# Low states on half the contraction rows: two heads of the state product side by side on TensorE, and a new order plan

## The chip, the cores and the metric

The kernel runs on one core of a Trainium2 chip. The metric is device time in microseconds (us) of one execution; the kernel before has a median of 700.57 us over 3 runs (700.18 to 702.35). The core has TensorE (PE in the profile, its weight loads on a row of their own, PEld), VectorE (DVE), ScalarE (ACT), GpSimd (POOL, almost unused here) and the queue of SyncE (SP), which issues all DMAs.

## The reference, cut to what matters

```python
B, H, S, Ns, D = 8, 8, 512, 32, 64          # x: B,H,S,D   state: B,H,Ns,D
a     = softmax(scale * x @ state^T)         # over the 32 states
xread = a @ state
a2    = softmax(scale * state @ x^T)         # over the 512 tokens
sread = a2 @ x
x     = concat([xread, sread], axis=2)       # 544 tokens a batch, 8 heads x 64
out   = ((x @ w_a) * (x @ w_b)) @ w_out      # 512 -> 1536 -> 512, float32
```

`xread @ w_a` is never formed through `xread`. Since `xread = a @ state`, the kernel multiplies the states of every head by that head's 64 rows of `w_a` and `w_b` first (the **state product**) and lets the attention weights `a` act on the result. The state product is what the change touches.

## The kernel before, in words

**Precision.** A float32 operand is split into a high part in TensorE's fast one-pass format (fp32r) and a low part, the rest. A product of two split operands is then three matmuls (high by high, high by low, low by high).

**Chunks.** The 1536 hidden columns are six chunks of 256. For each chunk, `w_a` and `w_b` together are 512 columns (the index `x` below). `weights(c, hp)` loads the 128 rows of a pair `hp` of heads (4 pairs) as raw 8-byte values, and `Conv` turns them into high and low float32 parts: one ACT `mul`, five DVE instructions, and copies into the tile `wq` of 128 rows by 2 heads by 512. In `conv_w`, head 0's high part stands in rows 64 to 127 and its low part in rows 0 to 63 of `wq[:, 0]`; head 1's high part stands in rows 64 to 127 and its low part in rows 0 to 63 of `wq[:, 1]`. The states (`sd_h` high, `sd_l` low) stand twice, in rows 0 to 63 and again in rows 64 to 127, so one matmul over all 128 rows adds (state times high weight) and (state times low weight).

**The state product.** `project(c, hp, bg, hh)` makes, for one head `hh` and one group `bg` of four batches, two such matmuls (`sd_h`, then `sd_l`) into one PSUM bank, `ms`; ACT copies the bank to SBUF, and after the second head two DMAs write the pair to scratch in DRAM (`scr`). The `sd_l` matmul of 128 rows also adds low state times low weight. `ms` has two banks, shared with the attention's small products. Each of the chunks 1 to 5 has 16 `project` calls (4 pairs, 2 heads, 2 groups) of two 512-column matmuls; chunk 0 is held in another layout, with 256-column matmuls.

**The MLP.** For a batch and 128 hidden columns, `layer1` reads the state product back (`p_raw<-scr`), splits it (`p_h`, `p_l`) and multiplies with the attention weights (`at_h`, `at_l`) into two `ab` banks; ACT and DVE multiply the two halves and split the result (`g_h`, `g_l`); `layer2` multiplies with `w_out` into four `acc` banks. `VISITS` says which batch takes which chunks in which order, since chunks become ready one after another.

**What sets the order.** Nothing runs in the order in which it is written. A `Recorder` notes all instructions as units (a `with rec.together` block is one unit, whose matmuls follow each other), `Recorder.cost` gives each unit a cost, and `plan` lists them by due times. Due times go backwards from a pace that the MLP's matmuls set, and `SHIFTS` (unit number: hundreds of ns) moves single units. The resulting order of each engine is fixed in the program.

Of the kernel before, what the change touches and what calls it, by code (L numbers as in the profile page):

```python
# [10 lines left out]
F32 = mybir.dt.float32  # L11
F32R = mybir.dt.float32r
# [8 lines left out]
P = 128  # L21
# [24 lines left out]
WIDE = (0, 1)  # L46

JOINED = 3

# [118 lines left out]
class Recorder:  # L168
# [31 lines left out]
    def cost(self, u, eng, method, out, ins, kw):  # L200
        n = 1
        sh = (out if isinstance(out, View) else ins[0]).where()[0]
        for x in sh[1:]:
            n *= x
        ps = bool(ins) and ins[0].tile.pool.name.startswith("ps")
        if eng == "PE":
            if method == "transpose" or kw.get("is_transpose"):
                o = n * .85
            elif ins[-1].dtype == F32R:
                o = (n + 32) / 2.4  # L210
            else:
                o = n / .6
            if sh[0] < P:
                o *= sh[0] / P
            if method == "matmul" and "is_transpose" not in kw and ins[-1].dtype == F32 and not u.turned:
                o, u.turned = o + 370, True
            lat = o + 172
        elif eng == "ACT":
            if method == "activation":
                o, lat = (870, 960) if "accum_out" in kw else (560, 660)  # L220
            elif ps:
                o, lat = 466 * n / 512 + (60 if n < 300 else 0), 587 * n / 512 + (80 if n < 300 else 0)
            else:
                o, lat = 522 * n / 512, 100 + n * 1.015
            if n < 8:
                o, lat = 60, 80
        elif eng == "DVE":
            if method.startswith("tensor_scalar") and not ps:
                o, lat = (65, 140) if n <= 1 else (75, 166) if n <= 16 else (333 * n / 512, 419 * n / 512)
            elif method == "tensor_reduce":  # L230
                o, lat = 593, 676
            elif method == "transpose":
                o, lat = 628, 704
            elif method == "reciprocal":
                o, lat = (72, 154) if n == 1 else (162, 244)
            else:
                o, lat = 65 + n * 1.045, 155 + n * 1.045
        elif eng == "SP":
            o = 440
            v = out if isinstance(out, View) else ins[0]  # L240
            u.bytes = 4
            for x in v.where()[0]:
                u.bytes *= x
            u.load = isinstance(out, View) and out.tile.pool.name != "dram"
            u.serve, u.land = u.bytes / 428 + (0 if u.load or u.bytes < 4e5 else 240), 1560 if u.load else 900
            lat = 980 + u.serve + u.land
        else:
            o, lat = 1000, 1060
        if eng in ("ACT", "DVE") and out.tile.name.startswith("sd_") and len(out.where()[0]) == 4:
            o, lat = 2 * o, 2 * lat  # L250
        if eng in ("ACT", "DVE"):
            o, lat = o * SLACK, lat * SLACK
        if u.calls[:-1]:
            u.lat = u.occ + lat
            u.occ += o
        else:
            u.occ, u.lat = o, lat
# [8 lines left out]
class Engine:  # L266
# [13 lines left out]


SHIFTS = {
# [12 lines left out]
}  # L295


# [164 lines left out]
def attn_moe(ctx, tc, xt, xn, sd, wl, w_out, out):  # L462
    base = tc.nc
    rec = Recorder()
# [7 lines left out]
    def pool(name, bufs, free=False, **kw):  # L472
        p = Pool(ctx.enter_context(tc.tile_pool(name=name, bufs=bufs, **kw)), name, bufs, free)
        pools.append(p)
        return p
# [4 lines left out]
    proj = pool("proj", 2)  # L480
# [8 lines left out]
    def f32(ap):  # L489
        return ap.bitcast(F32)  # L490
# [28 lines left out]
    class Conv:  # L519
# [15 lines left out]
        def run(self):  # L535
            raw, t1 = self.raw, self.t1
            his, los = self.parts()
            t2 = proj.tile([P, 512], I32, name="t2")
            nc.vector.tensor_scalar(out=t2, in0=t1, scalar1=3, scalar2=0x7FFFF000,
                                    op0=ALU.logical_shift_left, op1=ALU.bitwise_and)  # L540
            nc.vector.scalar_tensor_tensor(out=t2, in0=raw[:, :, 1], scalar=-(1 << 31), in1=t2,
                                           op0=ALU.bitwise_and, op1=ALU.bitwise_or)
            for rows, o in his[:1]:
                nc.scalar.copy(out=o, in_=f32(t2[rows]))

            nc.vector.tensor_scalar(out=t1, in0=t1, scalar1=3, scalar2=0xFFF,
                                    op0=ALU.logical_shift_left, op1=ALU.bitwise_and)
            nc.vector.scalar_tensor_tensor(out=f32(t1), in0=raw[:, :, 0].bitcast(U32), scalar=2.0 ** -29,
                                           in1=t1, op0=ALU.mult, op1=ALU.add)
            pw = raw.rearrange("p a b -> p (a b)")[:, :512]  # L550
            nc.vector.tensor_scalar(out=pw, in0=t2, scalar1=-(1 << 23), scalar2=None, op0=ALU.bitwise_and)
            for rows, o in los[:1]:
                nc.vector.scalar_tensor_tensor(out=o, in0=f32(t1[rows]), scalar=2.0 ** -23,
                                               in1=f32(pw[rows]), op0=ALU.mult, op1=ALU.mult)
            for o, i in los[1:]:
                nc.scalar.copy(out=o, in_=f32(i))
            for rows, o in his[1:]:
                nc.scalar.copy(out=o, in_=f32(t2[rows]))

    nxt = []  # L560


    LO, HI, ALL = slice(0, D), slice(D, P), slice(0, P)

    sd_h = [proj.tile([P, 4, 2, P], F32R, name=f"sd_h{j}", bufs=1) for j in range(2)]
    sd_l = [proj.tile([P, 4, 2, P], F32R, name=f"sd_l{j}", bufs=1) for j in range(2)]
# [16 lines left out]
    scr = [[dram.tile([NG, 4, 4, NS, 512], F32, name=f"scr{c}_{g}") for g in range(2)] for c in range(NC)]  # L583
    w = {}

    def conv_w(src, *key):


        def parts():
            t = w[key] = proj.tile([P, 2, 512], F32R, name="wq", bufs=4)  # L590
            return ((HI, t[HI, 1]), (LO, t[HI, 0])), ((ALL, t[:, 0]), (t[LO, 1], t[HI, 0]))
        return Conv(src, parts, 2)

    def weights(c, hp):

        if c:
            return conv_w(wl[2 * c:2 * c + 2, :, hp, :].rearrange("f p x -> p f x"), c, hp)
        f, g = hp // 2, hp % 2
        return conv_w(wl[f, :, 2 * g:2 * g + 2, :], 0, f, g)

# [6 lines left out]

    st = {"n": 0}
    SW = ("sw_st", 2), ("wo10", 1), ("sw_st", 2), ("wo11", 1)

    def project(c, hp, bg, hh, psp, tag):
        if hh == 0:
            name, bufs = SW[st["n"] % len(SW)]
            st[bg], st["n"] = proj.tile([P, 2, 512], F32, name=name, bufs=bufs), st["n"] + 1
# [179 lines left out]
    class Batch:  # L794
        n, nk = S, NG
# [80 lines left out]
    class States:  # L876
        n, nk, begun = B * NS, 4, False
# [127 lines left out]
    def attend(b):  # L1005
        if b not in a_t:
            new_a(b)
        for g in range(NG):
            a = atts[b, g]
            a.load()  # L1010
            if b >= JOINED:
                end_reads(a.scores)
# [27 lines left out]

    def products(c, bg, where=ms):
        for hp in range(4):
            for hh in range(2):
                project(c, hp, bg, hh, *where)
        flush()
# [79 lines left out]
    order, start = plan(rec.units, pools, T0)  # L1125
# [46 lines left out]
```

## Time and profile before

| | |
|---|---|
| median of 3 runs | 700.57 us |
| the profiled execution's own time | 700.03 us |
| its span in the profile | 698.2 us |
| PE busy | 677.7 us (97%), 3712 instructions |
| DVE busy | 486.5 us (70%), 947 instructions |
| ACT busy | 394.3 us (56%), 727 instructions |
| granted TensorE clock | 0.999 |
| DMA | 134.36 MB, mean 192 GB/s |

The span is the time from the first to the last instruction; the execution's own time is 1.8 us longer, for what lies around it. PE's busy share counts the modelled length of each matmul (about 0.39 us for 512 columns) where successive matmuls start 0.23 us apart, so a busy PE is read from the starts of its matmuls. All instructions are issued from one helper line (L1129 before, L1162 after), so groups are told apart by the names of tiles: `ms<-wq,sd_l` is a state product with low states, `ab<-...` is layer 1, `acc<-wo,...` layer 2, `ms<-x_raw` and `ms<-x_nat,a` are attention's products. A form such as `128*32` is rows by columns of the weights that the matmul uses.

### The profile page before, as it was taken

The page shows a single profiled execution, that of the slowest core. Times are in us where ns is not written, and L with a number is a line of the kernel's source. Part 1 is how long each engine was busy: PE and PEld are TensorE (multiplying, and loading weights), DVE is VectorE, ACT ScalarE, POOL GpSimd, SP SyncE. Part 2 cuts the span into 40 slices and gives each one's busy share as a digit, 9 for nine tenths or more (in the row PEclk, how much of TensorE's full clock was granted, in tenths as well). Part 3 has the DMA queues.
Part 4 walks back from the last instruction along what each step waited for, and adds up shares of the span by engine and source line. Part 5 has one row for each costly group of instructions (what it writes and reads, how often), then busy time and mean ns, then how long its engine had stood idle before and what let it go on. Part 6 is the DMA issues. An engine that isn't in the chain of part 4 may idle for free.

```text
span 698.2 us, 10183 instructions
## 1 busy us (share of the span) xinstructions
PE 677.7 (97%) x3712; PEld 543.2 (78%) x3712; DVE 486.5 (70%) x947; ACT 394.3 (56%) x727; POOL 0.7 (0%) x6
## 2 busy tenths in 40 slices
PE   4899999999999999999999999999999999999997
PEld 1576767887878888788888877877798888988886
DVE  5999788889986775745997367558869734884321
ACT  6988967898764667754543344334555433552322
POOL 0000000000000000000000000000000000000000
PEclk9999999999999999999999999999999999999999
DMA  8689977899495757768995144234244312500002
GB/s 325 243 295 336 338 248 243 307 319 393 163 335 204 271 171 251 252 232 263 392 332 158 59 155 125 95 120 139 82 152 150 109 43 61 181 31 30 1 0 92
DMA packets 55090, 134.36 MB, mean 192 GB/s; under 512 B 5632, under 2 KB 5632, under 8 KB 55040
## 3 DMA queue, kind: packets, MB, share of 16 engines
q1 hardware_dynamic: 55040, 133.71, 55.1%
q8 instruction: 29, 0.48, 0.3%
q14 instruction: 21, 0.17, 0.1%
HBM read 87.03 MB, written 46.66 MB: 191 GB/s over the span
## 4 chain that ended last, share of the span: by engine, by line
PE 88%; ACT 5%; DMA 5%; issue 1%; SPq 1%; DVE 0%; DVEq 0%
PE ab L1129 41%; PE acc L1129 38%; PE ms L1129 9%; ACT wq L1129 2%; DMA p_raw<-scr 1%; DMA p_raw<-sd 1%; DMA scr<-sw_st 1%; DMA part<-stg 1%; DMA scr<-wo 1%; SPq L1129 1%; ACT t L1129 1%; ACT sd_h L1129 0%; ACT wo L1129 0%; ACT sw_st L1129 0%; ACT g_h L1129 0%
## 5 line engine op out<-in xcount | busy, mean ns | idle before, releaser
L1129 PE MATMUL acc<-wo,g_h 128*128 128x512 f32 x816 | 249.0, 392 | 0.0
L1129 PEld LDWEIGHTS acc<-wo,g_h 128*128 128x128 f32 x816 | 151.6, 188 | 31.7 <-issue 0.8
L1129 DVE TENSOR_TENSOR a_sb<-ab,a_sb 128x512 f32<-128x512 f32 (+1 forms) x108 | 71.2, 659 | 130.2 <-PE ab L1129 115.2
L1129 PE MATMUL ab<-at_h,p_h 128*128 128x512 f32 x384 | 149.7, 394 | 2.4 <-ACT p_h L1129 2.4
L1129 PE MATMUL acc<-wo,g_l 128*128 128x512 f32 x408 | 150.9, 392 | 0.0
L1129 PE MATMUL ab<-at_l,p_h 128*128 128x512 f32 x384 | 149.6, 393 | 0.0
L1129 PE MATMUL ab<-at_h,p_l 128*128 128x512 f32 x384 | 148.8, 392 | 0.0
L1129 ACT COPY a_sb<-ab 128x512 f32<-128x512 f32 (+1 forms) x108 | 61.0, 565 | 137.6 <-PE ab L1129 137.0
L1129 ACT CAST g_h<-a_sb 128x512 fp32r<-128x512 f32 (+1 forms) x108 | 64.7, 599 | 59.5 <-DVE a_sb L1129 50.1
L1129 PEld LDWEIGHTS acc<-wo,g_l 128*128 128x128 f32 x408 | 76.6, 188 | 19.1 <-issue 2.5
L1129 DVE TENSOR_TENSOR g_l<-a_sb,g_h 128x512 fp32r<-128x512 f32 (+1 forms) x108 | 70.7, 655 | 28.1 <-ACT g_h L1129 21.3
L1129 PEld LDWEIGHTS ab<-at_h,p_h 128*128 128x128 f32 x384 | 72.2, 189 | 23.2 <-ACT p_h L1129 3.5
L1129 PEld LDWEIGHTS ab<-at_h,p_l 128*128 128x128 f32 x384 | 72.3, 189 | 16.0 <-issue 0.8
L1129 PEld LDWEIGHTS ab<-at_l,p_h 128*128 128x128 f32 x384 | 72.2, 189 | 15.3 <-issue 0.8
L1129 ACT CAST p_h<-p_raw 128x512 fp32r<-128x512 f32 x92 | 53.4, 621 | 24.5 <-PE ab L1129 16.0
L1129 DVE TENSOR_TENSOR p_l<-p_raw,p_h 128x512 fp32r<-128x512 f32 x92 | 60.1, 682 | 6.0 <-ACT p_h L1129 5.8
L1129 DVE TENSOR_SCALAR t<-t 128x512 int32<-128x512 int32 x120 | 49.6, 420 | 13.4 <-ACT t L1129 10.8
L1129 ACT CAST wq<-t 64x512 fp32r<-64x512 f32 (+1 forms) x64 | 38.7, 619 | 4.4 <-PE ab L1129 1.7
L1129 DVE SCALAR_TENSOR_TENSOR t<-raw,t 128x512 int32<-128x512 int32 (+1 forms) x60 | 39.5, 684 | 0.2
L1129 PE MATMUL ms<-wq,sd_h 128*128 128x512 f32 (+2 forms) x112 | 38.0, 412 | 0.3 <-ACT a L1129 0.2
L1129 PE MATMUL ms<-wq,sd_l 128*128 128x512 f32 (+2 forms) x112 | 37.4, 403 | 0.0
L1129 DVE TENSOR_TENSOR stg<-acc,stg 128x512 f32<-128x512 f32 x44 | 28.4, 683 | 9.2 <-PE acc L1129 9.2
(97 smaller groups left out, 671.4 us busy)
## 6 DMA issues: line engine op xcount, KB each, us to landing
p_raw<-scr SPq DMA_DIRECT2D x46, 512.0 KB, 4.0
scr<-sw_st SPq DMA_DIRECT2D x48, 256.0 KB, 5.1
scr<-wo SPq DMA_DIRECT2D x48, 256.0 KB, 4.2
raw<-wl SPq DMA_DIRECT2D x22, 512.0 KB, 6.1
part<-stg SPq DMA_DIRECT2D x20, 512.0 KB, 5.6
stg<-part SPq DMA_DIRECT2D x20, 512.0 KB, 5.0
out<-stg SPq DMA_DIRECT2D x34, 256.0 KB, 2.1
x_raw<-xt SPq DMA_DIRECT2D x14, 576.0 KB, 4.0
```

The lines of the kernel that those rows point to most:

```text
L1129: getattr(obj, method)(*map(real, args), **{k: real(x) for k, x in kw.items()})
```

## The change

Three things are changed.

1. **The state product from chunk 2 on** (`ROWS = 2`). `project_pair` takes both heads of a pair in one unit of four matmuls: two `sd_h` matmuls over all 128 rows, as before, and then two `sd_l` matmuls over 64 rows each: head 0's high weights with the low states in rows 0 to 63, head 1's in rows 64 to 127. The two are built for the upper and the lower 64 rows of TensorE (tile size 64 by 128, positions 0 and 64); low state times low weight is left out. The unit holds both `ms` banks at once, and both are copied after it. There are 4 chunks x 4 pairs x 2 groups = 32 such units.
2. **The conversion for these chunks** (`conv_rows`). Each head's high part now stands in the rows in which it was loaded, and the low part in the other head's rows. DVE writes the two low parts with one instruction of 64 rows each, in place of one of 128 rows; the ACT copy that moved a low part to the other rows is gone.
3. **The plan.** `Recorder.cost` halves the cost of a matmul whose contraction has under 128 rows, and all of `SHIFTS` is new, for the start of the kernel as well.

```diff
+ROWS = 2
...
             if sh[0] < P:
                 o *= sh[0] / P
+            elif method == "matmul" and ins[-1].where()[0][0] < P:
+                o /= 2
...
 SHIFTS = {
-    2: -1852, 7: 155, 8: 101, 12: 125, 13: -1927, 18: -166, 24: 194, 25: 125, 27: 16, 28: -291, 35: 29, 36: 59,
...
+    1: -25592, 2: -252, 3: -5612, 10: -253, 11: -298, 13: -13465, 14: -6031, 15: 585, 18: -5702, 24: -41270, 25:
...
-            for rows, o in los[:1]:
+            moved = [x for x in los if x[0] not in (LO, HI, ALL)]
+            for rows, o in los[:len(los) - len(moved)]:
                 nc.vector.scalar_tensor_tensor(out=o, in0=f32(t1[rows]), scalar=2.0 ** -23,
                                                in1=f32(pw[rows]), op0=ALU.mult, op1=ALU.mult)
-            for o, i in los[1:]:
+            for o, i in moved:
                 nc.scalar.copy(out=o, in_=f32(i))
...
+    def conv_rows(src, *key):
+
+        def parts():
+            t = w[key] = proj.tile([P, 2, 512], F32R, name="wq", bufs=4)
+            return ((LO, t[LO, 0]), (HI, t[HI, 1])), ((LO, t[HI, 0]), (HI, t[LO, 1]))
+        return Conv(src, parts, 2)
...
-            return conv_w(wl[2 * c:2 * c + 2, :, hp, :].rearrange("f p x -> p f x"), c, hp)
+            return (conv_rows if c >= ROWS else conv_w)(wl[2 * c:2 * c + 2, :, hp, :].rearrange("f p x -> p f x"), c, hp)
...
+    def project_pair(c, hp, bg, psp, tag):
+        name, bufs = SW[st["n"] % len(SW)]
+        sw, st["n"] = proj.tile([P, 2, 512], F32, name=name, bufs=bufs), st["n"] + 1
+        ps = [psp.tile([P, 512], F32, name=tag) for _ in range(2)]
+        h = 2 * (hp % 2)
+        with rec.together(sw):
+            for hh in range(2):
+                nc.tensor.matmul(ps[hh], lhsT=sd_h[hp // 2][:, h + hh, bg], rhs=w[c, hp][:, hh], start=True, stop=False)
+            for hh, rows in enumerate((LO, HI)):
+                nc.tensor.matmul(ps[hh], lhsT=sd_l[hp // 2][rows, h + hh, bg], rhs=w[c, hp][rows, hh],
+                                 start=False, stop=True)
+        for hh in range(2):
+            nc.scalar.copy(out=sw[:, hh], in_=ps[hh])
+        nxt.extend(...)          # the same two DMAs to scr
...
     def products(c, bg, where=ms):
         for hp in range(4):
+            if c >= ROWS:
+                project_pair(c, hp, bg, *where)
+                continue
             for hh in range(2):
                 project(c, hp, bg, hh, *where)
```

What this does to the order is seen at three places. On PE, the first state product of chunk 2 in each program, before (`ms_1626`, `ms_1632` are the two banks, `wq_1518` the weights of the first pair of heads):

```order
L1129 MATMUL acc_1613<-wo2_1080,g_l_1479 128x512
L1129 MATMUL ab_1623<-at_h_1422,p_h_1411 128x512
L1129 MATMUL ms_1626<-wq_1518,sd_h0_156 128x512
L1129 MATMUL ms_1626<-wq_1518,sd_l0_188 128x512
L1129 MATMUL ms_1632<-wq_1518,sd_h0_156 128x512
L1129 MATMUL ms_1632<-wq_1518,sd_l0_188 128x512
L1129 MATMUL ab_1623<-at_l_1443,p_h_1411 128x512
L1129 MATMUL ab_1623<-at_h_1422,p_l_1425 128x512
```

and after (`ms_1609` and `ms_1611`, weights `wq_1492`):

```order
L1162 MATMUL ab_1597<-at_h_1407,p_l_1434 128x512
L1162 MATMUL ab_1597<-at_h_1407,p_h_1420 128x512
L1162 MATMUL ms_1609<-wq_1492,sd_h0_114 128x512
L1162 MATMUL ms_1611<-wq_1492,sd_h0_114 128x512
L1162 MATMUL ms_1609<-wq_1492,sd_l0_119 128x512
L1162 MATMUL ms_1611<-wq_1492,sd_l0_119 128x512
L1162 MATMUL ab_1597<-at_l_1424,p_h_1420 128x512
L1162 MATMUL ab_1597<-at_h_1407,p_l_1434 128x512
```

The two `sd_l` matmuls now stand next to each other, with ordinary matmuls of 128 rows on either side; all 32 units stand so, with at least 10 other matmuls between one and the next.

On ACT, the conversion of that pair's weights before (two pairs, `wq_1518` and `wq_1524`, in turn; `t2` is the high part):

```order
L1129 CAST wq_1518<-t2_1122 64x512
L1129 CAST wq_1524<-t2_1159 64x512
L1129 COPY sw_st_1492<-ms_1504 128x512
L1129 CAST wq_1518<-wq_1518 64x512
L1129 ACTIVATE t1_1541<-wo8_1108 128x512
L1129 CAST wq_1524<-wq_1524 64x512
L1129 CAST wq_1518<-t2_1122 64x512
L1129 CAST wq_1524<-t2_1159 64x512
```

and after, where the copy from `wq` to `wq` is gone and two casts from `t2` are left:

```order
L1162 COPY sw_st_1473<-ms_1475 128x512
L1162 CAST wq_1492<-t2_1141 64x512
L1162 COPY a_sb_1497<-ab_1457 128x512
L1162 CAST wq_1492<-t2_1141 64x512
L1162 CAST p_h_1509<-p_raw_1350 128x512
```

On the SP queue, the first DMAs of the kernel before (`x_raw` is the first attention input, `raw` and `wo` raw weights, `p_raw<-sd` the states):

```order
L1129 DMA x_raw<-xt 128x1152
L1129 DMA raw<-wl 128x1024 x2
L1129 DMA stg<-xt 128x2x512
L1129 DMA stg<-xt 128x2x64
L1129 DMA p_raw<-sd 128x1024 x2
L1129 DMA wo_110<-wl 128x1024
```

and after:

```order
L1162 DMA p_raw<-sd 128x1024
L1162 DMA raw<-wl 128x1024
L1162 DMA x_raw<-xt 128x1152
L1162 DMA raw<-wl 128x1024
L1162 DMA wo_104<-wl 128x1024
L1162 DMA stg<-xt 128x2x512
L1162 DMA stg<-xt 128x2x64
L1162 DMA x_nat<-xn 128x1024
L1162 DMA p_raw<-sd 128x1024
```

The first half of the states has moved from fifth place to first, ahead of the first attention input, and the second half from sixth to ninth.

More of the change, by code (lines that the diff above doesn't have):

```diff
@@ L609, in attn_moe @@
     SW = ("sw_st", 2), ("wo10", 1), ("sw_st", 2), ("wo11", 1)
+    def project_pair(c, hp, bg, psp, tag):
[11 more added lines that the diff above has]
+            nc.scalar.copy(out=sw[:, hh], in_=ps[hh])
+        nxt.extend(lambda i=i: nc.sync.dma_start(
+            out=scr[c][bg][hp // 2, :, h + i].rearrange("b n x -> n b x"), in_=sw[:, i]) for i in range(2))
     def project(c, hp, bg, hh, psp, tag):
```

24 rows, old and new, of the table SHIFTS are left out of this document.

## The prediction, made before the change was run

> **What bounds the kernel now.** I read the page's head first, then the stretches of time, then what PE waits for.
>
> ```profile
> span 698.2 us, 10183 instructions
> PE 677.7 (97%) x3712; PEld 543.2 (78%) x3712; DVE 486.5 (70%) x947; ACT 394.3 (56%) x727; POOL 0.7 (0%) x6
> PE   4899999999999999999999999999999999999997
> PE 88%; ACT 5%; DMA 5%; issue 1%; SPq 1%; DVE 0%; DVEq 0%
> ```
>
> PE carries 88% of the chain that ended last and is full in all slices but those at the two ends. How full, by stretches (busy time per engine):
>
> ```profile
> 0.00:8.00 8.00, 1.93 (x8) 0.20 (x8) 0.09 (x1) 2.38 (x4) 0.70 (x6) 1.00 0.73 236
> 8.00:60.00 52.00, 43.20 (x351) 28.52 (x351) 49.61 (x114) 43.97 (x86) 0.00 (x0) 1.00 0.84 307
> 60.00:110.00 50.00, 48.79 (x339) 34.25 (x338) 41.84 (x87) 40.61 (x76) 0.00 (x0) 1.00 0.81 285
> 110.00:200.00 90.00, 90.00 (x467) 72.68 (x468) 78.42 (x155) 74.67 (x140) 0.00 (x0) 1.00 0.83 289
> 200.00:698.00 498.00, 493.80 (x2551) 407.52 (x2549) 316.54 (x594) 232.72 (x426) 0.00 (x0) 1.00 0.45 153
> ```
>
> The columns are length, PE, PEld, DVE, ACT, POOL, clock, DMA. Until 60 us DVE is the full engine (49.6 of 52); from 110 us it is PE. What PE waits for from 110 to 694 us is one row:
>
> ```profile
> PE ab L1129 <- ACT p_h L1129: 0.4, 1, 0.4
> ```
>
> So behind 110 us the kernel is as long as the sum of PE's steps. The products of chunks 2 to 5 lie there (the first start at 137 us, below), and a nanosecond more or less per matmul shows in full. Ahead of it, DVE and ACT decide.
>
> **PE, the saving.** The first state products of chunk 2 between layer matmuls, and from the view of the tile `ms` the lengths of attention's products (least, median, most, in ns):
>
> ```profile
> 137.23 0.39 PE L1129 MATMUL ms<-wq,sd_h 128*128 128x512 f32 x1
> 137.46 0.39 PE L1129 MATMUL ms<-wq,sd_l 128*128 128x512 f32 x1
> 137.68 0.39 PE L1129 MATMUL ms<-wq,sd_h 128*128 128x512 f32 x1
> 137.91 0.39 PE L1129 MATMUL ms<-wq,sd_l 128*128 128x512 f32 x1
> 138.14 0.39 PE L1129 MATMUL ab<-at_l,p_h 128*128 128x512 f32 x1
> ...
> L1129 PE MATMUL ms<-x_raw x112: 589/592/1061, 4.2 to 493.6; 128*32 128x512 f32 x112
> ```
>
> Four steps from 137.23 to 138.14 are 0.91 us: 0.2275 us a matmul; the length of 0.39 is 0.23 of streaming and 0.16 of tail. If the two 64-row matmuls stream at the same time, a unit saves one step less the small offset between tiles (about 0.007 us: four side by side take 0.61, row at 412.28 below, where the median of one is 0.592), 0.22 us; 32 units save 7.0 us.
>
> **PE, the price of the tile switch.** The new matmuls use another tile size than their neighbours. No 64-row matmul is in the trace, but attention's products use a tile size of 128 by 32, four side by side. One such excursion, in and out:
>
> ```profile
> 410.83 0.39 PE L1129 MATMUL ab<-at_l,p_h 128*128 128x512 f32 x1
> 411.06 0.39 PE L1129 MATMUL ab<-at_h,p_l 128*128 128x512 f32 x1
> 411.38 0.26 PE L1129 MATMUL ms<-x_nat,a 128*32 128x64 f32 x3
> ...
> 412.28 0.61 PE L1129 MATMUL ms<-x_raw 128*32 128x512 f32 x4
> 412.82 0.50 PE L1129 MATMUL ab<-at_h,p_h 128*128 128x512 f32 x1
> 413.16 0.39 PE L1129 MATMUL ab<-at_l,p_h 128*128 128x512 f32 x1
> 413.39 0.39 PE L1129 MATMUL ab<-at_h,p_l 128*128 128x512 f32 x1
> ```
>
> In: 411.06 to 411.38 is 0.32, against 0.23 between neighbours, 0.09 late. Out: the last four end at 412.89; less the tail of 0.16 the array was free at 412.73, and the next starts at 412.82, 0.09 late; its follower comes 0.34 later, not 0.23, another 0.11. That 0.11 is a weight load which nothing hides:
>
> ```profile
> 412.82 0.19 PEld L1129 LDWEIGHTS ab<-at_h,p_h 128*128 128x128 f32 x1 [0.84 <-issue]
> 412.93 0.19 PEld L1129 LDWEIGHTS ab<-at_l,p_h 128*128 128x128 f32 x1
> 413.16 0.19 PEld L1129 LDWEIGHTS ab<-at_h,p_l 128*128 128x128 f32 x1
> ```
>
> In the steady stream a load starts together with the matmul ahead of the one that it serves; across the switch it does not, and the second load follows the first by 0.11, the time of 128 columns. Attention's products are also of another type (plain float32), so type could be the reason; transposes of that type, with the full tile, say no:
>
> ```profile
> 408.08 0.39 PE L1129 MATMUL acc<-wo,g_h 128*128 128x512 f32 x1
> 408.31 0.60 PE L1129 MATMUL ms<-ident,e 128*128 128x128 f32 x4
> 408.67 0.47 PE L1129 MATMUL acc<-wo,g_h 128*128 128x512 f32 x1
> 408.98 0.39 PE L1129 MATMUL acc<-wo,g_l 128*128 128x512 f32 x1
> ```
>
> They begin 0.23 after their forerunner, with no delay. The delay goes with the tile size. The Trainium skill states it as a rule ("TensorEngine Tiling (Array Packing)", section Key Properties): a change of the tiling mode, not of the tile within one, drains the TensorE, and it counts 64 by 128 as a mode of its own. By that rule the rows above carry over to the change; the trace agrees for 128 by 32, and no run shows it for 64 rows.
>
> Price of one unit: 0.09 in, 0.09 + 0.11 out, and on the way in a load of 128 columns that nothing hides, 0.11: 0.40 us. Less the 0.22 saved, that is +0.18 us a unit and +5.8 us for 32. Bounds if there is a switch: without the load on the way in 0.29 - 0.22, +2.2 us; with the two 64-row loads one behind the other 0.51 - 0.22, +9.3 us. I take +5.8, since all loads of the exit rows have 128 columns, as the new ones do, and the four loads of a 128 by 32 group are issued together.
>
> **Conversion and banks.** Groups by form, for what is dropped and added:
>
> ```profile
> L1129 ACT CAST wq<-wq 64x512 fp32r<-64x512 f32 x24 | 14.8, 619 | 0.4
> L1129 ACT CAST wq<-t 128x512 fp32r<-128x512 f32 x16 | 9.8, 623 | 3.5 <-PE ab L1129 1.7 <-DVE t L1129 1.6
> L1129 DVE SCALAR_TENSOR_TENSOR wq<-t,raw 128x512 fp32r<-128x512 f32 x22 | 14.8, 685 | 1.8 <-PE ms L1129 1.6
> L1129 ACT COPY sw_st<-ms 128x512 f32<-128x512 f32 x44 | 25.1, 594 | 9.2 <-PE ms L1129 9.0
> ```
>
> 16 of the 24 ACT copies go: -9.9 us of ACT, which is not the bound. 16 DVE instructions come; ACT's 64-row copies take what 128-row ones take (619 against 623 ns), so I cost them like the 128-row row, 0.685 us: +11.0 us of DVE. Eight of them (5.5 us) fall near 110 to 200 us, where DVE has 90.0 - 78.4 = 11.6 us idle, the others where it has 181 us idle. Cost 0, with up to +2 us if the idle time is in the wrong places; then PE would wait ahead of `ms<-wq`.
>
> A unit takes both `ms` banks, and the next needs both copies, 2 x 0.59 us. Ten matmuls between units are 2.3 us. Cost 0; attention's products, which share the banks, come late before PE does.
>
> **The start.** The order brings the states first. Before:
>
> ```profile
> 4.25 1.93 PE L1129 MATMUL ms<-x_raw 128*32 128x512 f32 x8 [4.25 <-DMA x_raw<-xt]
> 7.22 0.66 ACT L1129 ACTIVATE t<-raw 128x512 f32<-128x512 f32 x1 [4.88 <-DMA raw<-wl]
> 7.91 0.43 DVE L1129 TENSOR_SCALAR t<-t 128x512 int32<-128x512 int32 x1 [7.91 <-ACT t L1129]
> 11.65 1.15 ACT L1129 CAST sd_h<-p_raw 128x512 fp32r<-128x512 f32 x1 [0.34 <-DMA p_raw<-sd]
> 16.24 1.10 DVE L1129 TENSOR_TENSOR sd_l<-p_raw,sd_h 128x512 fp32r<-128x512 f32 x1
> ```
>
> The first DMA has landed by 4.25 us. With the states there, ACT can make two casts (2.3 us) and DVE two subtractions (2.2 us) ahead of 7.9 us, where DVE now stands idle, and DVE is the full engine up to 60 us: at most -2.2 us. Against it the attention input comes third; the second landing is at 7.2 us, so the scores start about 3 us later, and if that chain decides, the start costs +3. DVE being the fuller, I take -1.5 us.
>
> **The sum.** Against the profiled execution (span 698.2 and 1.8 around it, 700.0): 700.0 + 5.8 - 1.5 = 704.3. The median of the runs shown, 700.57, is 0.5 above that execution, so I forecast 704.8 us. Own range of this case: 700.0 + 2.2 - 2.2 + 0.5 = 700.5 up to 700.0 + 9.3 + 0 + 0.5, about 710.
>
> **Rivals.**
> *No switch cost: 64-row tiles mix freely with full ones.* The mechanism: the two row halves take their weights in the shadow of the matmul ahead, as full loads do now (PEld starts with the matmul before). For it speaks that row tiles leave the columns as they are, where 128 by 32 splits them; against it the rows at 411.38 and 412.82. Time: 700.0 - 7.0 - 1.5 + 0.5 = 692.0 us, from 689 to 695. It decides as soon as a unit's price in and out falls under 0.22 us. The Trainium skill has a page on this side too ("TensorE: Matmul & The Clock Gate", Part 3): it gives four 32-row tiles side by side 3.07 times the speed of one after another. By that page alone the pair streams together, which both cases take; it measured no change between modes.
> *No pairing: the two matmuls run one after the other*, so the change doesn't do what it says. Four 128 by 32 tiles that start within 0.02 us speak against it. Without a switch cost 700.5 - 1.5 = 699.0; with it another 7.0 on the forecast, near 712.
> *DVE or the shared banks become the bound* between 110 and 200 us: idle time there falls from 11.6 to 6 us. It adds its +2 us or more to the forecast, 707 and up.
>
> **How the numbers follow.** Switch cost with pairing 0.50, no switch cost 0.36, no pairing 0.07 (0.04 with, 0.03 without switch), DVE or banks on top 0.07. A difference under 0.3%, 2.1 us, is about what a measurement of this kernel can't tell from none. Faster (under 698.5): the 0.36, and some 0.03 from a start that gains more: 0.39. Same (to 702.7): the lower part of the forecast's own range, 0.15, and the unpaired case without a switch, 0.03: 0.18. Slower: the rest, 0.43. The range runs from 690 to 709: it takes in both signs, and leaves out the no-pairing case with a switch and the tails.
>
> **What would show it.** After: the row `ms<-wq,sd_l` in two forms, 64 of them with 64 rows, their starts within 0.01 us in pairs. If I am right, the first of a pair starts about 0.3 us behind its forerunner, not 0.23, and the full matmuls behind it carry some 0.2 us; `ms<-wq,sd_h` starts stay 0.23 apart; PE's waits behind 110 us stay under 1 us; DVE's busy time is near 497. If starts around the pairs show no delay, the step of the price is wrong and 7 us come off. A wait of PE on DVE `wq` or ACT `sw_st` would show the cover gone, and more idle PE ahead of 110 us than before would make the start's sign wrong.

## The result, and the profile after

The changed kernel takes 706.39 us in the median (704.22 to 706.86, 5 runs), the kernel before 700.57 us (699.49 to 702.35, 5 runs): ratio 1.0066, 95% interval 1.0039 to 1.0093. It is slower by 0.7%, 5.8 us. The profiled execution took 705.19 us with a span of 703.4.

The head of the page, as before:

```profile
span 703.4 us, 10173 instructions
PE 683.1 (97%) x3712; PEld 534.2 (76%) x3712; DVE 498.7 (71%) x963; ACT 385.7 (55%) x711; POOL 0.7 (0%) x6
PE   3899999999999999999999999999999999999997
PE 91%; ACT 4%; DMA 3%; SPq 1%; issue 0%; DVE 0%; DVEq 0%; ACTq 0%
```

PE has as many instructions as before, and its busy time is up by 5.4 us; the chain lies on PE for 91%, not 88%. DVE has 16 more instructions and 12.2 us more, ACT 16 fewer and 8.6 us less. By stretches (length, PE, PEld, DVE, ACT, POOL, clock, DMA):

```profile
8.00:60.00 52.00, 45.28 (x362) 28.62 (x363) 47.38 (x110) 44.92 (x89) 0.00 (x0) 0.93 0.85 308
60.00:110.00 50.00, 48.28 (x339) 34.01 (x337) 42.92 (x91) 38.05 (x71) 0.00 (x0) 1.00 0.82 281
110.00:200.00 90.00, 90.00 (x423) 68.10 (x420) 73.82 (x137) 62.95 (x117) 0.00 (x0) 1.00 0.82 285
200.00:703.00 503.00, 499.38 (x2595) 403.39 (x2593) 332.43 (x626) 235.69 (x431) 0.00 (x0) 1.00 0.45 152
```

From 110 us on PE is as full as before, and the view of waits has no row at all for PE between 110 and 699 us (0.4 us before). Nothing makes PE wait for another engine, so its own steps must have become longer. The counts don't show it: of the 44 instructions fewer between 110 and 200 us (423, before 467), 40 are small products of attention that fall outside this stretch here. The timeline of PE around one unit shows it, and the weight loads beside it (start, length, instruction):

```profile
145.71 0.39 PE L1162 MATMUL ab<-at_h,p_l 128*128 128x512 f32 x1
145.94 0.61 PE L1162 MATMUL ms<-wq,sd_h 128*128 128x512 f32 x2
146.48 0.50 PE L1162 MATMUL ms<-wq,sd_l 64*128 64x512 f32 x2
146.91 0.50 PE L1162 MATMUL ab<-at_h,p_h 128*128 128x512 f32 x1
147.25 0.39 PE L1162 MATMUL ab<-at_l,p_h 128*128 128x512 f32 x1
147.48 0.40 PE L1162 MATMUL ab<-at_h,p_l 128*128 128x512 f32 x1
```

```profile
146.48 0.19 PEld L1162 LDWEIGHTS ms<-wq,sd_l 64*128 64x128 f32 x2 [0.35 <-issue]
146.91 0.19 PEld L1162 LDWEIGHTS ab<-at_h,p_h 128*128 128x128 f32 x1 [0.24 <-issue]
147.02 0.19 PEld L1162 LDWEIGHTS ab<-at_l,p_h 128*128 128x128 f32 x1
```

The two 64-row matmuls start together (their starts are 0.003 to 0.004 us apart) and stream side by side. But the first starts 0.318 us behind the second `sd_h`, not 0.227; the next full matmul starts 0.43 us behind the pair, where a pair that streams needs 0.227; and its follower comes another 0.34 later. The loads say why: the load for the pair starts with the pair (146.48), not with the matmul ahead, so it delays the pair. The load for the next full matmul starts only with that matmul too (146.91); the load after it follows 0.11 later (147.02), the time of one load, and so this 0.11 is not hidden either. Medians over the 32 units are 0.318, 0.003, 0.428 and 0.338 us, in all 1.087 us where four steps of 0.227 are 0.908.

### The profile page after: what moved, and what is told of

The parts are those of the page before. It is cut to its first block, busy times and chain, and to the rows that moved or that the text cites. A ratio compares the mean times of both kernels' runs of the same rounds, so it can differ in the third digit from the quotient of the medians.

```text
span 703.4 us, 10173 instructions
## 1 busy us (share of the span) xinstructions
PE 683.1 (97%) x3712; PEld 534.2 (76%) x3712; DVE 498.7 (71%) x963; ACT 385.7 (55%) x711; POOL 0.7 (0%) x6
## 4 chain that ended last, share of the span: by engine, by line
PE 91%; ACT 4%; DMA 3%; SPq 1%; issue 0%; DVE 0%; DVEq 0%; ACTq 0%
PE ab L1162 42%; PE acc L1162 40%; PE ms L1162 10%; DMA p_raw<-sd 1%; ACT wq L1162 1%; DMA scr<-wo 1%; SPq L1162 1%; DMA p_raw<-scr 1%; ACT p_h L1162 0%; ACT stg L1162 0%; ACT a L1162 0%; ACT wo L1162 0%; ACT e L1162 0%; ACT t L1162 0%; ACT at_l L1162 0%
## 5 line engine op out<-in xcount | busy, mean ns | idle before, releaser
L1162 PE MATMUL acc<-wo,g_h 128*128 128x512 f32 x816 | 255.2, 393 | 0.0
L1162 PE MATMUL acc<-wo,g_l 128*128 128x512 f32 x408 | 156.2, 392 | 0.0
L1162 PE MATMUL ab<-at_h,p_h 128*128 128x512 f32 x384 | 152.0, 398 | 1.9 <-ACT p_h L1162 1.6
L1162 DVE TENSOR_TENSOR g_l<-a_sb,g_h 128x512 fp32r<-128x512 f32 (+1 forms) x108 | 70.8, 655 | 16.5 <-ACT g_h L1162 16.3
L1162 ACT CAST p_h<-p_raw 128x512 fp32r<-128x512 f32 x92 | 53.4, 623 | 15.9 <-PE ab L1162 9.8
L1162 ACT COPY wo<-ms 128x512 f32<-128x512 f32 x44 | 24.3, 592 | 16.0 <-PE ms L1162 13.1
L1162 PE MATMUL ms<-wq,sd_h 128*128 128x512 f32 (+2 forms) x112 | 32.5, 409 | 0.0
```

The lines of the kernel that those rows point to most:

```text
L1162: getattr(obj, method)(*map(real, args), **{k: real(x) for k, x in kw.items()})
```

## The experiments

Two theories stood. **Switch theory:** every change between the full tile and the 64-by-128 tile, in and out, costs PE about 0.1 us before the next matmul can begin (called drain below) and 0.11 us of a weight load that nothing hides, together more than the 0.22 us that the pairing saves. **Plan theory:** the order that the new `SHIFTS` make costs the time, or DVE and the shared `ms` banks under it. In e1 to e3, e6 and e8 every engine's instructions stand in the order of the changed kernel (the costs in the plan were held, by lines not shown here), so that only the edited matmuls differ.

### e1 and e6: the low states over all 128 rows again

```diff
-            for hh, rows in enumerate((LO, HI)):
-                nc.tensor.matmul(ps[hh], lhsT=sd_l[hp // 2][rows, h + hh, bg], rhs=w[c, hp][rows, hh], ...)
+            for hh in range(2):
+                nc.tensor.matmul(ps[hh], lhsT=sd_l[hp // 2][:, h + hh, bg], rhs=w[c, hp][:, hh], ...)
```

> The changed kernel with one thing undone: the two low-state matmuls of a unit run over all 128 rows again (full tile); conversion, plan and the order of every engine stay as in the changed kernel. Switch theory: a unit goes from 0.318 + 0.004 + 0.427 + 0.338 = 1.087 us back to 4 x 0.227 = 0.908 us, 32 x 0.179 = 5.7 us come off: about 700.7 us, no different from the kernel before. Plan theory (the new order costs the time): stays near 706.4 us. Theory of DVE or the banks: stays near 706 us too, since both copies and all DVE instructions are still there.

Measured: 698.94 us beside 700.63 for the kernel before (ratio 0.9973, interval 0.9953 to 0.9993). The cost is gone, with the new plan, the new conversion, both copies and both banks still in place, so the plan theory falls. In e1's trace the unit reads as the prediction's rows of before do:

```profile
146.75 0.61 PE L1164 MATMUL ms<-wq,sd_h 128*128 128x512 f32 x2
147.21 0.62 PE L1164 MATMUL ms<-wq,sd_l 128*128 128x512 f32 x2
147.66 0.39 PE L1164 MATMUL ab<-at_h,p_h 128*128 128x512 f32 x1
147.89 0.39 PE L1164 MATMUL ab<-at_l,p_h 128*128 128x512 f32 x1
```

The distance to the changed kernel was 7.5 us, more than the 5.7 expected. Set against each other matmul by matmul, the two traces differ not only by the four steps: behind the three long steps four or five more are 0.228 to 0.236 us, until the matmuls are back at 0.227. From the start of a unit to the tenth matmul behind it the mean is 3.147 us in the changed kernel and 2.943 in e1: 0.203 us a unit, 6.5 us for 32. To see whether that is all, both were run once more, on one chip:

> The low-state matmuls over all 128 rows once more, same orders. Plan theory for the start (the states first let ACT and DVE begin earlier, -1.5 us): 0.5 to 2.5 us below the kernel before again, near 699.3 us. If the first time was chance: 700.6 us, no difference.

Measured: 699.76 us beside 699.99 (0.9996, interval 0.9981 to 1.0011): this time no difference to the kernel before. So the new plan with its start and the new conversion, without the pairs, is worth -1.7 us in one set of runs and -0.2 us in the other; it is not settled to better than that.

### e5: the changed kernel beside it

No edit.

> The changed kernel as it is, beside the next ones on the same chip. Its trace against that of full rows gives 0.203 us a unit from the start of the unit to the tenth matmul behind it (3.147 against 2.943 us), 6.5 us for 32. Switch theory: 6.5 us over full rows in this job, about 706 where full rows is 699.5. A theory by which part of the earlier distance of 7.5 us came from another cause than the units would show a distance under 5 or over 8 us here as well.

Measured: 705.81 us (1.0085, interval 1.0068 to 1.0102), 6.05 us over e6 on the same chip, against 6.5 from the steps.

### e2: one tile of the two

```diff
-            for hh, rows in enumerate((LO, HI)):
-                nc.tensor.matmul(ps[hh], lhsT=sd_l[hp // 2][rows, h + hh, bg], rhs=w[c, hp][rows, hh], ...)
+            nc.tensor.matmul(ps[0], lhsT=sd_l[hp // 2][LO, h, bg], rhs=w[c, hp][LO, 0], ...)
```

Head 1's low-state part is left out; its `sd_h` matmul closes its bank.

> The changed kernel with only the first of the two 64-row matmuls of each unit (head 1's low-state part is left out), all orders the same. Switch theory with pairing: the second matmul streams beside the first and is worth its 0.004 us offset, 0.1 us in all: 706.3 us, within 0.5 of the changed kernel. If the two streamed one after the other and the trace's starts deceived: 32 x 0.22 = 7.0 us come off, 699.4 us.

Measured: 704.83 us (1.0053, interval 1.0035 to 1.0070), 1.5 us under the 706.3 expected. Half the 64-row matmuls are gone, and no 7 us come off. The tiles do run side by side:

```profile
147.57 0.61 PE L1161 MATMUL ms<-wq,sd_h 128*128 128x512 f32 x2
148.11 0.50 PE L1161 MATMUL ms<-wq,sd_l 64*128 64x512 f32 x1
148.54 0.50 PE L1161 MATMUL ab<-at_h,p_h 128*128 128x512 f32 x1
148.88 0.39 PE L1161 MATMUL ab<-at_l,p_h 128*128 128x512 f32 x1
```

One tile makes the same excursion: in the medians 0.318 from the second `sd_h` to the tile, 0.428 to the next full matmul, 0.333 to its follower. The expectation of 0.1 us was too small all the same: by the traces a unit is 0.028 us shorter, 0.9 us for 32, since the matmuls behind a single tile are back at 0.227 after these steps.

### e3: the pair twice

```diff
+            for k in range(2):
                 for hh, rows in enumerate((LO, HI)):
-                    ...  start=False, stop=True)
+                    ...  start=False, stop=(k == 1))
```

> The changed kernel with the pair of 64-row matmuls issued twice in each unit (the low-state part is added twice), all orders the same. If the price hangs on the switch in and out: the second pair adds one streaming step, 0.22 to 0.23 us a unit, 32 x 0.227 = 7.3 us: 713.7 us. If it hangs on every 64-row matmul or its weight load (0.11 each that nothing hides): 0.33 us a unit or more, 10.7 us and up: 717 us or above.

Measured: 713.39 us (1.0163, interval 1.0133 to 1.0194), against 713.7 for a price that hangs on the switch.

```profile
147.81 0.61 PE L1165 MATMUL ms<-wq,sd_h 128*128 128x512 f32 x2
148.36 0.73 PE L1165 MATMUL ms<-wq,sd_l 64*128 64x512 f32 x4
149.02 0.50 PE L1165 MATMUL ab<-at_h,p_h 128*128 128x512 f32 x1
149.35 0.39 PE L1165 MATMUL ab<-at_l,p_h 128*128 128x512 f32 x1
```

The median steps are 0.318 in, 0.003, 0.332 to the second pair, 0.003, 0.323 out, 0.338. The first pair alone has 0.428 to the next matmul. From the start of a unit to the tenth matmul behind it e3 takes 3.382 us, the changed kernel 3.147: a second pair within the same mode (tile size) adds 0.235 us, about one streaming step. The steps also show what the 0.428 holds: 0.332 is 0.227 plus the first pair's load of 0.105; 0.323 is 0.227 plus a drain of 0.096.

### e8: every second unit

```diff
+            for hh, rows in enumerate((LO, HI) if hp % 2 else (ALL, ALL)):
```

> The changed kernel with the 64-row pair in every second unit only (16 of 32), full rows in the others, orders the same. Switch theory: every unit pays for itself alone, half of the distance between full rows and the changed kernel, 16 x 0.203 = 3.2 us over full rows, near 702.7 us. If the cost came once (from the mode being used at all, or from where the units stand): not half, but nearly all or nothing.

Measured: 702.85 us (1.0043, interval 1.0030 to 1.0057), 3.1 us over e6 on the same chip: 16 units, half of e5's 6.05. Each unit pays for itself.

### e7: the conversion of before

```diff
-            return (conv_rows if c >= ROWS else conv_w)(wl[2 * c:2 * c + 2, :, hp, :]..., c, hp)
+            return conv_w(wl[2 * c:2 * c + 2, :, hp, :]..., c, hp)
```

> Full rows, and the conversion of before too (one DVE instruction of 128 rows and a third ACT copy in place of two DVE instructions of 64 rows): 11 us less DVE, 10 us more ACT; some 100 rows of each engine's order shift. If DVE's 11 us are hidden, as the prediction took it: within 1 us of full rows. If DVE or its order costs time between 110 and 200 us: 1 to 2 us faster than full rows.

Measured: 701.89 us (1.0025, interval 1.0011 to 1.0039), 2.1 us slower than e6, which neither case foresaw. The difference lies ahead of the units: the first unit of chunk 2 starts at 139.4 us, in e6 at 137.8, while from there to the last matmul both take 557.9 to 558.0 us. DVE is 12 us less busy in e7 and that changes nothing from there on. From 110 to 350 us e6 has (length, PE, PEld, DVE, ACT, POOL, clock, DMA)

```profile
110.00:200.00 90.00, 90.00 (x465) 72.72 (x465) 75.97 (x140) 64.93 (x122) 0.00 (x0) 1.00 0.82 285
200.00:350.00 150.00, 149.87 (x698) 122.70 (x697) 117.30 (x217) 92.27 (x167) 0.00 (x0) 1.00 0.76 265
```

so with the new conversion in DVE still has 14 and 33 us idle, and PE none and 0.1. The 11 us are hidden. Why the start is slower in e7 (another order, or a stretch from 60.8 to 64.2 us in which its profile has the clock at half) is open, since its order of instructions differs in places.

### e4: the first attention input first

```diff
     order, start = plan(rec.units, pools, T0)
+    sp = [i for i in order if rec.units[i].eng == "SP"]
+    x = next(i for i in sp if any(t.name == "x_raw" for t, _, _ in rec.units[i].acc))
+    order.remove(x)
+    order.insert(order.index(sp[0]), x)
```

> The changed kernel with the first attention input issued first on the SP queue, ahead of the states, the only move. In the changed kernel PE begins at 7.9 us, not 4.2, and the granted clock falls to half from 23.5 to 30.3 us, which the kernel before doesn't show. If the late input is what eats the gain of the start: PE begins near 4.3 us, the clock stays full, and 1 to 2 us come off: about 705 us. If DVE and ACT decide the start: no change within 0.7 us, or up to 1 us slower as the casts of the states start later.

Measured: 708.56 us (1.0095, interval 1.0067 to 1.0123): slower than the changed kernel, by 2.0 us if the ratios are compared with the first measurement (1.0066) and by 0.7 us with e5 (1.0085); no run of the unedited kernel stands beside it on this chip. PE does begin early, and it helps nobody:

```profile
4.35 1.94 PE L1166 MATMUL ms<-x_raw 128*32 128x512 f32 x8 [4.35 <-DMA x_raw<-xt]
10.97 1.08 PE L1166 MATMUL ms<-ident,e 128*128 128x128 f32 x4 [4.69 <-ACT e L1166]
```

```profile
7.14 2.02 ACT L1166 CAST sd_h<-p_raw 128x512 fp32r<-128x512 f32 x2 [4.80 <-DMA p_raw<-sd]
8.97 1.39 ACT L1166 ACTIVATE t<-raw 128x512 f32<-128x512 f32 x2
10.25 0.58 ACT L1166 COPY e<-ms 128x512 f32<-128x512 f32 x1
```

ACT has the casts of the states first in its order and waits for the states until 7.14 us. In the changed kernel it casts from 4.70, and PE begins later:

```profile
4.70 2.02 ACT L1162 CAST sd_h<-p_raw 128x512 fp32r<-128x512 f32 x2 [2.36 <-DMA p_raw<-sd]
7.89 1.94 PE L1162 MATMUL ms<-x_raw 128*32 128x512 f32 x8 [7.89 <-DMA x_raw<-xt]
```

The first unit of chunk 2 starts at 138.7 us in e4, in e1, e2 and e3 (same chip, and up to there the same order but for this one DMA) at 136.5 to 137.1. By these starts the states' place is worth 1.6 to 2.2 us within this order. The clock falls to half in e4 as well (26.5 to 33.3 us), so the late input isn't what lets it fall. The expectation was wrong on the kernel before in one point: its record of the clock begins at 27.3 us only, and ahead of that its matmuls were slow too:

```profile
25.84 1.20 PE L1129 MATMUL ab<-at_l,p_h 128*128 128x512 f32 x2
26.84 0.83 PE L1129 MATMUL ab<-at_h,p_l 128*128 128x512 f32 x2
27.52 0.62 PE L1129 MATMUL ab<-at_h,p_h 128*128 128x512 f32 x2
```

Two 512-column matmuls take 1.20 us there and 0.62 from 27.5 us on.

## Why the prediction was right

- **What bounds the kernel.** Right: from 110 us on PE waits for nobody, and what a unit's steps gain or lose was found again in the time (e3, e8).
- **The saving** of 0.22 us by pairing. Right: the two tiles start 0.003 to 0.004 us apart, and e2 shows that they stream together. One part was missed: behind a pair the stream loses 0.028 us more than behind a single tile. That the pair's second load is the reason fits e2 but was not shown.
- **The price of the switch.** Right in its parts: 0.09 us late on the way in, 0.11 for the first load, 0.09 to 0.10 of drain on the way out, 0.11 for the load behind; 0.40 forecast from attention's 128-by-32 products, 0.403 in the medians of the steps (1.087 - 0.908, and the 0.224 saved). Mis-sized by what comes behind: with four or five slower steps a unit's net is +0.203, not +0.18, 6.5 us in place of 5.8.
- **The rule of the Trainium skill** in "TensorEngine Tiling (Array Packing)", Key Properties, that a change of tiling mode drains TensorE while tiles of one mode don't, agrees with the runs for 64 by 128: on the way out of a pair the next step is 0.323 us (e3), 0.096 more than the stream's 0.227, while from one pair to the next it is 0.332, the stream and one load.
- **Conversion and banks** at cost 0. Right from 110 us on: no wait of PE, and DVE's 11 us are idle time used. But they do not fall where the prediction put them. It had DVE's idle time between 110 and 200 us go from 11.6 to 6 us; it is 16.2 (90.0 - 73.8), and DVE is 15.9 us busier behind 200 us, in the new order. What e7 shows ahead of 110 us was not foreseen.
- **The start** at -1.5 us. Not settled. Within the new order the states' early place helps (e4), but against the kernel before e1 and e6 put the new plan with its start at -1.7 and -0.2 us. By the sign that the prediction set for itself, more idle PE ahead of 110 us, there is no gain at all: PE idles 16.3 us there (18.7 in e5, the same kernel), before 16.1. Of this 7.9 us, before 4.2, pass ahead of the first matmul.
- **The sum.** 704.8 us forecast, 706.39 measured: 0.7 us of the difference is the longer unit, and with the mean of -1.7 and -0.2, -1.0 in place of -1.5, another 0.5; 700.57 + 6.5 - 1.0 = 706.1. The range from 690 to 709 holds the 692.0 of "no switch cost" too, so a time inside it says little by itself; what bears the mechanism out is the price of each unit.
- **The rivals.** "No switch cost" is out by the rows at 146.48 and by e1, e3 and e8; "no pairing" by e2; "DVE or the banks" by e1, where both are in place.

No version here beats the kernel before beyond doubt: full rows under the new plan came out once at 0.9973 and once at 0.9996.

## What to carry to other kernels

Half-row tiles pay only if enough pairs follow each other. One way in and out costs about 0.40 us of PE and 0.02 more behind it, and a pair saves 0.22. By this estimate two pairs in one mode break even, and three or more win; no run here has shown a win. Before such a change, look in the trace for any other small tile and read the step in, the step out and the step behind it; here attention's products gave the price to within 0.03 us a unit. And where PE is the bound, read the distances between the starts of its matmuls and not its busy share: that is 97% both times, with 5 to 6 us between.

## What the runs showed of the hardware

- The switch costs the same in both shapes that these kernels have, 64 by 128 in fp32r and 128 by 32 in plain float32: 0.318 us on the way in for both, 0.34 for the follower on the way out. Other shapes were not run.
- Behind a switch out of a pair, and the follower's 0.338 us, the stream of 512-column matmuls has four or five steps of 0.228 to 0.236 us until it is back at 0.227 (six or seven in e3, with two pairs); behind a single tile (e2) it has none. Why is open.
- The loads of two 64-row tiles are issued 0.003 us apart and together cost what one load does: 0.332 us from the first pair to the second in e3, and 0.428 us to the next full matmul behind a pair and behind a single tile alike.
